# Two layers of attention and a routed feed-forward network: six additions of softmax tiles moved from GpSimd to VectorE, with four edits at the kernel's end

## The chip, the cores and the metric

The kernel runs on one core of one Trainium2 chip. The core has a matrix engine (TensorE, in the profile PE, with its weight loads shown as PEld), an elementwise engine (VectorE, DVE), an engine for activations (ScalarE, ACT), a general engine (GpSimd, POOL) and one that mostly issues transfers (SyncE, SP). Each works through its own list of instructions in order and waits on semaphores for the others. Sixteen DMA engines move data; SP, ACT and POOL issue transfers to them.

The metric is the device time of one execution in microseconds (us), lower is better. Three runs of the kernel before took 4557.66 to 4558.62 us, with a median of 4558.31.

## The reference

The input x has 2048 tokens of 1024 numbers. Two layers follow each other, with the same weights:

```python
    def _A_ref(x, wqkv, wo):
        ...                       # H = 32 heads of 32
        scores = jnp.einsum("bhqd,bhkd->bhqk", q, k) * scale
        p = _softmax(scores, axis=-1)
        o = jnp.einsum("bhqk,bhkd->bhqd", p, v)
        return (lambda x, *d: x.transpose(*d))(o, 0, 2, 1, 3).reshape(B, S, D) @ wo

    def _B_ref(x, w_r, w_gate, w_up, w_down):
        r = x @ w_r
        idx = jnp.argsort(-r, axis=-1)[:, :C]          # the 8 tokens with the largest r
        ...
        g = _silu(x_sel @ w_gate)
        u = x_sel @ w_up
        y = (g * u) @ w_down                           # 1024 -> 3584 -> 1024, 8 tokens only
        r_sel = _sigmoid(jnp.take_along_axis(r, idx, axis=1))
        y = y * r_sel.reshape(B, C, 1)
        ...                                            # y is added to those 8 rows
    x = x + _A_ref(_layernorm(x, axis=-1), A_wqkv, A_wo)
    x = x + _B_ref(_layernorm(x, axis=-1), B_w_r, B_w_gate, B_w_up, B_w_down)
    x = x + _A_ref(_layernorm(x, axis=-1), A_wqkv, A_wo)
    x = x + _B_ref(_layernorm(x, axis=-1), B_w_r, B_w_gate, B_w_up, B_w_down)
```

So each layer is full attention over 2048 tokens, then a router that picks 8 tokens for a gated feed-forward network.

## The kernel before, in words

**Attention.** After a normalisation and the projections, attention is cut into 32 units (8 groups of four heads, by 4 chunks of 512 queries). A unit has 16 steps, one for each tile of 128 keys, so there are 512 steps in a layer. A step computes scores (PE, L703), takes their exponential (ACT, L1099) into a tile P of 128 by 2048, and one or two steps later multiplies P with the values (PE, L1025). A separate product and reduction find each row's maximum ahead of time (PE L688, DVE L696); it runs 25 steps ahead of the exponentials, and so VectorE's large reductions end 25 steps before the last step.

**The softmax's sums.** The 16 P tiles of a unit must be summed. Five times a tile is added onto another by a transfer that accumulates, issued by GpSimd (`merge`, L1038). Eight tiles are added into a buffer `acc` by GpSimd (`acc_add`, L1035). At step 22 counted from the unit's start (in the next unit, `SUM_AT`) PE multiplies two P tiles and `acc` by ones (`sum_mm`, L1045), and ACT copies the result (L1055). When each of these happens is written in tables:

```python
MERGED = ((2, 0), (8, 6), (11, 8), (13, 10), (15, 12))
ADDED = ((5, 3), (6, 0), (9, 5), (12, 4), (14, 6), (15, 8), (16, 10), (20, 12))
```

The first number is the step from the unit's start, the second the tile; a merge adds the next tile onto it. Thus tiles 6, 8, 10 and 12 are added after their merges. P tiles live in nine buffers, and an exponential waits until its buffer's last reader is done. In the last unit of a layer there are no merges: VectorE makes 12 adds and three tiles go directly to the sum.

**Output projection.** It works in 16 row tiles of 128 tokens (PE L1238). Each tile t has a scaling of the attention output by the sums' reciprocals (`scale_o`, L1161 on VectorE, L1170 and L1173 for the split into two parts), the products, a sum with x (L1243), a normalisation (L1271) and the router's logits (L1273, which writes its product into the accumulator that the products came from). In layer 1 the last two row tiles, 14 and 15, are computed apart from the others (L1303) with parts of the router's work called in between; `row_sums` (L1312, L1315) and `logits` (L1320, L1321) finish them. The row tile 15 is scaled in row tile 12's turn.

**The routed network in layer 1.** `finish` runs 49 steps: eight gate steps and eight up steps for the first half of the network's width, a transposition (L548), the same for the second half, fourteen down steps (L563), and the output y (L578), which GpSimd scatters to the tokens' rows (L579). Gate and up products are L531. After each gate, up and down step SP issues the next weights' load (L204, L207). Gate results go through ACT (L538, L539), VectorE (L540, L541) and GpSimd (L542) before VectorE multiplies them with the up results (L544).

**The moving-back.** Some rows had been exchanged with others so that the router could work on a part of the tokens early. `back(i)` gathers eight rows (GpSimd, L216), loads eight others (ACT's queue) and scatters both groups (GpSimd, L220) to where they belong. In `choose`, `back(1)` is called at the end, which is after step 2; `back(0)` follows after step 9. GpSimd's queue takes these in program order.

Of the kernel before, what the change touches and what calls it, by code (L numbers as in the profile page):

```python
# [19 lines left out]
NT = S // 128  # L20
# [3 lines left out]
NU = NG * QC  # L24
# [13 lines left out]
ADDED = ((5, 3), (6, 0), (9, 5), (12, 4), (14, 6), (15, 8), (16, 10), (20, 12))  # L38
FIRST = 2
# [8 lines left out]
KEYS_AT[3, 3] = slice(3 * 512, S)  # L48


def unit_events(last):
    if last:
        return [(k + 1, "mid", 1, "add", (k, 0 if k == 1 else None, True)) for k in range(1, NT) if k not in LAST_DIRECT]
    ev = [(at, "end", 0, "merge", (k, k + 1)) for at, k in MERGED]
    ev += [(at, "end", 1, "add", (k, FIRST if at == ADDED[0][0] else None, False)) for at, k in ADDED]
    return ev + [(SUM_AT, "mid", 5, "sum", ())]


EVENTS = {False: unit_events(False), True: unit_events(True)}


@with_exitstack
def tile_kernel(ctx, tc, x, wqkv, wo, w_r, w_gate, w_up, w_down, out):
    nc = tc.nc
    sync, dve, act, pool, pe = nc.sync, nc.vector, nc.scalar, nc.gpsimd, nc.tensor
# [15 lines left out]
    def ps_st():  # L81
        return psum.tile([128, 512], F32, name="st", bufs=3)
# [4 lines left out]
    def ps_pv():  # L87
        return psum.tile([128, 512], F32, name="pv")
# [23 lines left out]
    pos = cons.tile([128, NT], F32, name="pos")  # L112
# [30 lines left out]
    def ln_stats(xt, st=None):  # L143
        if st is None:
            st = small.tile([128, 2, 6], F32, name="bst", bufs=3)
            for i in range(2):
                dve.bn_stats(st[:, i, :], xt[:, i * 512:(i + 1) * 512])
        mv = small.tile([128, 2], F32, name="mv", bufs=3)
        dve.bn_aggr(mv, st)  # L149
        rs = small.tile([128, 1], F32, name="rs", bufs=3)  # L150
        pool.tensor_tensor(rs, mv[:, 1:2], eps_c, op=OP.add)  # L151
        pool.tensor_tensor(rs, rs, mhalf, op=OP.pow)
        return mv, rs

    class FeedForward:
# [67 lines left out]
        def tiny(self, shape, name, dtype=F32):  # L223
            return small.tile(shape, dtype, name=name, bufs=1)
# [152 lines left out]
        def back(self, i):  # L377

            end, perm = (CUT + 8, S)[i], PERM[i]
            rows, last = (self.tmp.tile([128, D], F32, name=k, bufs=b)[0:8] for k, b in (("x", 3), ("wrb", 1)))  # L380
            self.gather(rows, perm["ab"][:, 1:2], self.dst)
            act.dma_start(last, self.dst[end - 8:end, :])
            self.scatter(perm["ab"][:, 0:1], rows, self.dst)
            self.scatter(perm["routed"], last, self.dst)

        def token(self, s):

            j = small.tile([64, 8], F32, name="tj")
            for i in (1, 0):
                a, b, t, bc = self.tiny([64, 1], "ta"), self.tiny([64, 1], "tb"), self.tiny([64, 1], f"tt{i}"), PERM[i]["bc"]  # L390
                dve.scalar_tensor_tensor(j, bc[:, 0:8], s, bc[:, 8:16], op0=OP.is_equal, op1=OP.mult, accum_out=a)
                dve.scalar_tensor_tensor(j, tails[i], s, bc[:, 16:24], op0=OP.is_equal, op1=OP.mult, accum_out=b)
                dve.tensor_tensor(a, a, b, op=OP.add)
                dve.tensor_tensor(t, a, s, op=OP.add)
                s = t
            return s
# [83 lines left out]
        def choose(self):  # L480

            tiny, f = self.tiny, self.final
            mx, mi, mif = tiny([1, 8], "mx1"), tiny([1, 8], "mi", U32), tiny([1, 8], "mif")
            dve.max(mx, f)
            dve.max_index(mi, mx, f)
            dve.tensor_copy(mif, mi)
            yield
            p = ps_st()
            pe.matmul(p[0:64, 0:8], ones_c[0:1, 0:64], mif, start=True, stop=True)
            tables = (self.cand, last_c[0], last_c[1])  # L490
            for j, t in enumerate(tables):
                pe.matmul(p[0:64, 16:25], self.pk[0:t.shape[0], j, :], t, start=(j == 0), stop=(j == 2))
            eq, away, tab = tiny([64, 8], "eq64"), tiny([64, 1], "away"), tiny([64, 9], "tab")
            dve.tensor_scalar(eq, p[0:64, 0:8], col_c, None, op0=OP.is_equal)
            dve.tensor_copy(tab, p[0:64, 16:25])
            dve.tensor_reduce(away, eq, axis=AX.X, op=OP.max)
            dve.tensor_scalar(away, away, -4.0 * S, 4.0 * S, op0=OP.mult, op1=OP.add)
            place, idx, tok = tiny([64, 1], "place64"), tiny([64, 1], "idx64", I32), tiny([64, 1], "tok64", I32)
            dve.scalar_tensor_tensor(place, tab[:, 0:1], 2.0, half_c, op0=OP.mult, op1=OP.add)
            dve.tensor_copy(idx, place)  # L500
            halves = self.halves = self.dst.rearrange("s (b c) -> (s b) c", b=2)
            self.gather(self.bg, idx, halves)

            t = self.token(tab[:, 0:1])
            dve.scalar_tensor_tensor(place, t, 2.0, half_c, op0=OP.mult, op1=OP.add)
            dve.tensor_tensor(place, place, away, op=OP.add)
            dve.tensor_copy(tok, place)
            self.tok = tok
            sg = self.sg = tiny([64, 1], "sg64")
            act.activation(sg, tab[:, 8:9], AF.Exp, scale=-1.0)  # L510
            dve.tensor_scalar(sg, sg, 1.0, None, op0=OP.add)
            dve.reciprocal(sg, sg)
            self.back(1)
            yield

        def row_tile(self):
# [2 lines left out]
        def step(self):  # L519
# [3 lines left out]
            k, h, a = u = self.steps.pop(0)  # L523
            nj = 4 - h
            m = 32 * nj
            if k in "gu":
                if a == 0:
                    self.acc = ps_pv()
                w = self.W.pop(u)
                for j in range(nj):  # L530
                    pe.matmul(self.acc[32 * j:32 * j + 32, :], self.xs[:, a, :], w[:, j * 512:(j + 1) * 512],  # L531
# [65 lines left out]
            self.lag = 0  # L597

        def finish(self):
            choice = self.choose()  # L600
            for i in range(len(self.steps)):
                if self.step():
                    if self.free:
                        self.pools.append(self.free.pop(0))
                    self.load()
                if i in (0, 2):
                    next(choice)
                if i == 9:
                    self.back(0)
            self.close()  # L610

        def close(self):
# [19 lines left out]
    def layer(n, src, dst, prev=None, following=None):  # L632
# [93 lines left out]
        with ExitStack() as pst:  # L726
# [209 lines left out]
            for k, (c, wb, i) in enumerate(steps):  # L936
# [26 lines left out]
                at = b - (1, 8)[c == 0]  # L963
                t = 4 * (c + 1) + at // 4
# [30 lines left out]
        with sbuf(f"at{n}", bufs=2) as aw:  # L995
# [79 lines left out]
            def emit(s, where):  # L1075
                u, kt = divmod(s, NT)
                todo = []
                for back in (1, 0):
                    v = u - back
                    if 0 <= v < NU:  # L1080
                        todo += [(kt + NT * back, pri, fn, args, v) for (k, pos, pri, fn, args) in EVENTS[v == NU - 1]
                                 if k == kt + NT * back and pos == where]
                for k, _, fn, args, v in sorted(todo, key=lambda e: (-e[0], e[1])):
                    fns[fn](v, *args)
# [5 lines left out]
            for s in range(NS + 14):  # L1090
                u, kt = divmod(s, NT)
# [10 lines left out]
                t = s - 1 if s < NS - LEAD else s - 2  # L1102
# [39 lines left out]
        if True:  # L1142
# [17 lines left out]
            def scale_o(t):  # L1160
                dve.tensor_tensor(OR[t], OR[t], RD.pop(t), op=OP.mult)  # L1161
# [61 lines left out]
            for t in range(NT - 2 if n else NT):  # L1223
# [27 lines left out]
                mv, rs = ln_stats(x2)  # L1251
                if low:
                    low()
                if n and t == NT - 4:
                    scale_o(NT - 1)
                if first_stage and t == CT + 3:
                    list(first_stage)
                    next(nxt)
# [12 lines left out]
                dve.tensor_scalar(xn, x2, mv[:, 0:1], rs, op0=OP.subtract, op1=OP.mult)  # L1271
                waste = wp.tile([128, D], F32, name="x", bufs=3) if nxt and t == NT - 1 else p
                dve.scalar_tensor_tensor(waste, xn, 1.0, wrb, op0=OP.mult, op1=OP.mult, accum_out=rcols[:, t:t + 1])  # L1273
                if nxt and NT - 3 <= t < NT - 1:
                    next(nxt)
                pool.tensor_tensor(x2, x2, xn, op=OP.add)
# [9 lines left out]
        if n:  # L1286

            parts = ffn.first_rows(rcols)
# [4 lines left out]
            todo = [(i, x, wol, a, both) for i, x in ((0, ah), (1, bh)) for a in range(KD)]  # L1293
# [14 lines left out]
            def row_sums(i, between=None):  # L1308
                st = small.tile([128, 2, 6], F32, name="bst", bufs=3)
                for h in both:  # L1310
                    o = x2s[i][:, halves[h]]
                    dve.tensor_tensor(o, p[i][h], o, op=OP.add)  # L1312
                    if between and h == 0:
                        next(between)
                    dve.bn_stats(st[:, h, :], o)  # L1315
                mvs[i], rss[i] = ln_stats(None, st)

            def logits(i):
# [12 lines left out]
            xns = [wp.tile([128, D], F32, name="xn", bufs=1), more[:, 0:D]]  # L1331
            last = [ffn.last_rows(1 + i, rcols[:, NT - 2 + i:NT - 1 + i], xns[i]) for i in both]
            row_sums(0)
            next(parts)
            pool.memset(ffn.pk, 0.0)
# [15 lines left out]
            for i in range(2):  # L1351
                t = NT - 2 + i
# [40 lines left out]
```

## Time and profile before

| | us |
|---|---|
| three runs, median (lowest to highest) | 4558.31 (4557.66 to 4558.62) |
| the profiled execution, its time | 4557.8 |
| its span, first to last instruction | 4556.0 |
| PE busy | 4506.4 |
| GpSimd busy | 3231.7 |
| VectorE busy | 3150.2 |
| ScalarE busy | 2428.5 |

A row of a timeline reads: start in the span, busy time, engine, line of the kernel, operation, what it writes and reads, how many instructions the row stands for, and in brackets how long the engine was idle before and what ended that. L numbers are lines of the kernel before. Names such as `ohl`, `wol`, `fw` or `xn` are buffers that serve several uses one after another; in the routed network they hold weights or intermediate results. Layer 1's attention ends near 4284 us and its routed network starts near 4478 us.

### The profile page before, as it was taken

To read this page: it belongs to the slowest core of one execution; us is meant where nothing else is said; L and a number is where in the kernel's file an instruction comes from. 1 tells how busy PE (TensorE), PEld (TensorE's weight loads), DVE (VectorE), ACT (ScalarE), POOL (GpSimd) and SP (SyncE) were. 2 spreads that over 40 slices of the span, in tenths; PEclk is the share of its full clock that TensorE was granted. 3 is DMA by queue.
4 is the path that set the end of the run, shared out by engine and by line. 5 is a ranking of instruction groups with operands and counts; after the bars stand their busy time and mean duration, and the time that the engine had idled before them with its cause. 6 is when DMAs were issued, how large, how long until landed. Compare 5 with 4: busy or idle time off the path is not lost.

```text
span 4556.0 us, 73559 instructions
## 1 busy us (share of the span) xinstructions
PE 4506.4 (99%) x29241; PEld 2686.4 (59%) x29241; DVE 3150.2 (69%) x4963; ACT 2428.5 (53%) x2574; POOL 3231.7 (71%) x1251
## 2 busy tenths in 40 slices
PE   9999999999999999999999999999999999999997
PEld 7888745555555555548877786555555555555583
DVE  2211588888888888876522225888888888888663
ACT  3322267767676767670222222767777676767510
POOL 4444378989898889855633343888989898989452
PEclk9999999999999999999999999999999999999998
DMA  6757477777777768758698774877777777777598
GB/s 206 210 171 207 130 170 154 171 156 160 167 163 158 172 145 180 168 122 242 183 318 279 252 207 122 175 153 166 164 152 174 157 160 167 164 158 175 140 277 322
DMA packets 329719, 833.62 MB, mean 183 GB/s; under 512 B 43996, under 2 KB 160732, under 8 KB 280206
## 3 DMA queue, kind: packets, MB, share of 16 engines
q1 hardware_dynamic: 275454, 476.43, 35.4%
q0 software_dynamic: 45248, 325.67, 35.3%
q10 hardware_dynamic: 8672, 26.81, 2.2%
q8 instruction: 230, 3.77, 0.3%
q14 instruction: 115, 0.94, 0.1%
HBM read 384.34 MB, written 119.47 MB: 111 GB/s over the span
## 4 chain that ended last, share of the span: by engine, by line
PE 94%; DMA 2%; POOL 1%; issue 1%; DVE 1%; ACT 0%; ACTq 0%; POOLq 0%; SPq 0%; DVEq 0%
PE pv L1025 22%; PE pre L703 21%; PE st L821 17%; PE st L688 16%; PE pre L821 6%; PE pre L1238 5%; PE st L1045 4%; POOL acc L1035 1%; PE pv L531 1%; PE pre L688 1%; PE pv L821 0%; PE pre L790 0%; DMA ord<-rd 0%; PE st L571 0%; PE pre L1303 0%
## 5 line engine op out<-in xcount | busy, mean ns | idle before, releaser
L696 DVE TENSOR_REDUCE nm<-st 128x1 f32<-128x512 f32 x3916 | 2434.0, 684 | 376.1 <-PE st L688 370.1
L1099 ACT ACTIVATE P<-pre 128x1024 f32<-128x1024 f32 x2048 | 1985.9, 1022 | 723.3 <-PE pre L703 521.4
L1035 POOL TENSOR_TENSOR acc<-acc,P 128x2048 f32<-128x2048 f32 x434 | 2103.9, 4848 | 86.2 <-DMA P<-P 75.4
L703 PE MATMUL pre<-q,ks 64*128 64x512 f32 (+1 forms) x8192 | 1142.4, 396 | 4.3 <-ACT P L1099 4.3
L1025 PE MATMUL pv<-P,v 128*32 128x512 f32 x8192 | 1092.8, 606 | 4.8 <-DMA v<-vd 4.8
L688 PEld LDWEIGHTS st<-ks,q 64*128 64x128 f32 x3916 | 547.0, 184 | 907.4 <-DVE nm L696 764.9
L688 PE MATMUL st<-ks,q 64*128 64x512 f32 x3916 | 985.9, 471 | 0.5
L703 PEld LDWEIGHTS pre<-q,ks 64*128 64x128 f32 (+1 forms) x8192 | 776.1, 187 | 186.0 <-ACT P L1099 57.4
L1038 POOL DMA_DIRECT2D P<-P x310 | 296.8, 957 | 260.0 <-PE st L688 189.3
L836 DVE TENSOR_TENSOR lo<-st,hi 128x512 fp32r<-128x512 f32 x128 | 88.4, 692 | 528.4 <-ACT hi L835 505.2
L756 POOL TENSOR_TENSOR ohl<-wraw,ord 128x2048 fp32r<-128x2048 f32 (+1 forms) x54 | 222.5, 4124 | 308.1 <-ACT ord L751 299.5
L756 POOL TENSOR_TENSOR wl<-wraw,wh 128x2048 fp32r<-128x2048 f32 (+1 forms) x54 | 222.4, 4122 | 303.7 <-ACT wh L755 284.9
L835 ACT CAST hi<-st 128x512 fp32r<-128x512 f32 x128 | 75.2, 587 | 496.5 <-PE st L821 493.3
L1025 PEld LDWEIGHTS pv<-P,v 128*32 128x32 f32 x8192 | 162.5, 108 | 261.3 <-issue 253.6
L1035 POOL TENSOR_TENSOR acc<-P 128x2048 f32<-128x2048 f32 x62 | 294.0, 4742 | 11.0 <-ACT P L1099 11.0
L1238 PE MATMUL pre<-woh,ohl 128*128 128x512 f32 x960 | 223.2, 390 | 0.0
L1238 PEld LDWEIGHTS pre<-woh,ohl 128*128 128x128 f32 x960 | 180.0, 188 | 39.6 <-ACT ohl L1170 1.7
L821 PE MATMUL st<-xh,wh 128*128 128x512 f32 x512 | 201.4, 393 | 0.0
L821 PE MATMUL st<-xh,wl 128*128 128x512 f32 x512 | 199.6, 390 | 0.0
L821 PE MATMUL st<-xl,wh 128*128 128x512 f32 x512 | 199.5, 390 | 0.0
L151 POOL TENSOR_TENSOR rs<-mv,eps_c 128x1 f32<-128x1 f32 x64 | 29.3, 457 | 232.2 <-DVE mv L149 232.2
L1170 ACT CAST ohl<-ord 128x1024 fp32r<-128x1024 f32 x32 | 33.6, 1052 | 269.9 <-DVE ord L1161 115.7
(384 smaller groups left out, 3995.7 us busy)
## 6 DMA issues: line engine op xcount, KB each, us to landing
P<-P POOLq DMA_DIRECT2D x310, 1024.0 KB, 8.8
wraw<-in_A_wqkv_dram SPq DMA_DIRECT2D x96, 1024.0 KB
q<-qh SPq DMA_DIRECT2D x256, 128.0 KB
ks<-kh SPq DMA_DIRECT2D x112, 256.0 KB
fw<-in_B_w_down_dram SPq DMA_DIRECT2D x17, 1024.0 KB
vd<-vn SPq DMA_DIRECT2D x32, 512.0 KB
qh<-hi SPq DMA_DIRECT2D x64, 256.0 KB
ql<-lo SPq DMA_DIRECT2D x64, 256.0 KB
```

Of the source, the lines that this page charges most:

```text
L688: pe.matmul(ps[b], Q[u][rows, i, 0, qt * 128:(qt + 1) * 128], KS[(u // QC) % 2][rows, i, 0, j * 512:(j + 1) * 512], start=True, stop=True, ...
L696: dve.tensor_reduce(NM[u][:, j, 2 * i + b:2 * i + b + 1, qt], ps[b], axis=AX.X, op=OP.max, negate=True)
L703: pe.matmul(p[:, b * 512:(b + 1) * 512], KS[(u // QC) % 2][rows, i, slot, kt * 128:(kt + 1) * 128], Q[u][rows, i, slot, :], start=(slot == ...
L756: pool.tensor_tensor(wl[:, sl], raw[:, sl], wh[:, sl].bitcast(F32), op=OP.subtract)
L821: pe.matmul(p, *pair(a, l, r), start=(a == 0 and k == 0), stop=(a == KD - 1 and k == 2))
L836: dve.tensor_tensor(lo, p, hi.bitcast(F32), op=OP.subtract)
L1025: pe.matmul(PV[u][32 * h:32 * h + 32, :], V[g][:, kt, 32 * h:32 * h + 32], P[s][:, h, :], start=(kt == 0), stop=(kt == NT - 1), tile_posit ...
L1035: (dve if on_dve else pool).tensor_tensor(o, a, P[u * NT + k].rearrange("p h c -> p (h c)"), op=OP.add)
L1038: pool.dma_start(P[u * NT + a], P[u * NT + b], accum_op=OP.add)
L1045: pe.matmul(p[32 * h:32 * h + 32, :], ones32, a[:, h, :], start=(i == 0), stop=(i == len(parts) - 1), tile_position=(0, 32 * h))
L1099: act.activation(P[s][:, 2 * i:2 * i + 2, :].rearrange("p h c -> p (h c)"), p, AF.Exp, scale=SCALE)
L1238: pe.matmul(p[:, bl], l[:, a, :], r[a][:, bl], start=(k == 0 and a == 0), stop=(k == 2 and a == KD - 1))
```

## The change

1. `unit_events` takes the number of units that are left. For the last unit but one (`left == 1`), the adds at steps 9 and later, six of eight, are made by VectorE instead of GpSimd. This holds in both layers.
2. `back` becomes a generator with two parts (gather and load; scatters). `choose` no longer calls it. `finish` runs `back(1)`'s parts after steps 3 and 8, and `back(0)`'s after steps 17 and 25.
3. In layer 1, the up steps accumulate in the pool `ps_st` instead of `ps_pv`, which the gate steps use.
4. In layer 1, `scale_o` of row tile 15 moves behind row tile 12's normalisation and logits.
5. In `row_sums`, each half's statistics are taken directly after its sum, ahead of the router's part that is called in between.

```diff
+ON_DVE = 9
...
-def unit_events(last):
-    if last:
+def unit_events(left):
+
+    if left == 0:
         return [(k + 1, "mid", 1, "add", (k, 0 if k == 1 else None, True)) for k in range(1, NT) if k not in LAST_DIRECT]
     ev = [(at, "end", 0, "merge", (k, k + 1)) for at, k in MERGED]
-    ev += [(at, "end", 1, "add", (k, FIRST if at == ADDED[0][0] else None, False)) for at, k in ADDED]
+    ev += [(at, "end", 1, "add", (k, FIRST if at == ADDED[0][0] else None, left == 1 and at >= ON_DVE)) for at, k in ADDED]
     return ev + [(SUM_AT, "mid", 5, "sum", ())]
...
-EVENTS = {False: unit_events(False), True: unit_events(True)}
+EVENTS = [unit_events(i) for i in range(3)]
...
             act.dma_start(last, self.dst[end - 8:end, :])
+            yield
             self.scatter(perm["ab"][:, 0:1], rows, self.dst)
             self.scatter(perm["routed"], last, self.dst)
+            yield
...
             dve.reciprocal(sg, sg)
-            self.back(1)
             yield
...
                 if a == 0:
-                    self.acc = ps_pv()
+                    self.acc = ps_st() if self.n and k == "u" else ps_pv()
...
         def finish(self):
-            choice = self.choose()
+            choice, backs = self.choose(), [self.back(i) for i in range(2)]
+
+            parts = {0: choice, 2: choice, 3: backs[1], 8: backs[1], 17: backs[0], 25: backs[0]}
             for i in range(len(self.steps)):
...
-                if i in (0, 2):
-                    next(choice)
-                if i == 9:
-                    self.back(0)
+                if i in parts:
+                    next(parts[i])
...
-                        todo += [(kt + NT * back, pri, fn, args, v) for (k, pos, pri, fn, args) in EVENTS[v == NU - 1]
+                        todo += [(kt + NT * back, pri, fn, args, v) for (k, pos, pri, fn, args) in EVENTS[min(NU - 1 - v, 2)]
...
-                if n and t == NT - 4:
-                    scale_o(NT - 1)
...
                 dve.scalar_tensor_tensor(waste, xn, 1.0, wrb, op0=OP.mult, op1=OP.mult, accum_out=rcols[:, t:t + 1])
+                if n and t == NT - 4:
+                    scale_o(NT - 1)
...
                     dve.tensor_tensor(o, p[i][h], o, op=OP.add)
+                    dve.bn_stats(st[:, h, :], o)
                     if between and h == 0:
                         next(between)
-                    dve.bn_stats(st[:, h, :], o)
```

## The prediction

> **What bounds the kernel now.** I read the page first, then a table of the engines' work by stretches of the span, then the instruction rows of each engine around the places that the diff touches. The page gives the span and says which engine carries the end.
>
> ```profile
> span 4556.0 us, 73559 instructions
> PE 4506.4 (99%) x29241; PEld 2686.4 (59%) x29241; DVE 3150.2 (69%) x4963; ACT 2428.5 (53%) x2574; POOL 3231.7 (71%) x1251
> PE 94%; DMA 2%; POOL 1%; issue 1%; DVE 1%; ACT 0%; ACTq 0%; POOLq 0%; SPq 0%; DVEq 0%
> ```
>
> TensorE is busy 4506.4 of 4556.0 us, so only some 50 us can be won by removing waits, and a removed wait pays only if TensorE has no other wait behind it. The table by stretches shows where that holds (stretch, length, busy time of PE, PEld, DVE, ACT and POOL, granted clock, DMA share, GB/s).
>
> ```profile
> 4288.00:4440.00 152.00, 152.00 (x670) 125.36 (x668) 104.56 (x128) 20.15 (x20) 73.59 (x91) 1.00 0.94 261
> 4475.00:4500.00 25.00, 20.06 (x149) 7.30 (x148) 7.45 (x30) 1.28 (x3) 6.29 (x7) 0.84 0.86 309
> 4500.00:4530.00 30.00, 24.95 (x142) 7.27 (x144) 6.40 (x6) 1.06 (x2) 6.05 (x6) 0.89 1.03 400
> ```
>
> Layer 1's output projection (4288 to 4440) has no gap in PE: what attention gains ahead of it arrives behind it. In the routed network at the end (from 4475) PE has gaps, and from 4500 the DMA engines have none: there the weights' transfers bound the work, not PE.
>
> **Attention, layer 0.** The rows of PE, then of ScalarE, then of GpSimd in time order around the last unit but one's sum, then one unit's sum without a wait from the chain of work, and layer 1's two rows that frame the same place:
>
> ```profile
> 1998.77 1.38 PE L703 MATMUL pre<-q,ks 64*128 64x512 f32 x8
> ...
> 2002.03 0.74 PE L703 MATMUL pre<-q,ks 64*128 64x512 f32 x4 [0.88 <-ACT P L1099]
> ...
> 2004.50 1.90 PE L1045 MATMUL st<-P,ones 128*32 128x512 f32 x16
> 2007.53 1.07 PE L1045 MATMUL st<-acc,ones 128*32 128x512 f32 x8 [1.13 <-POOL acc L1035]
> ...
> 2011.17 1.38 PE L703 MATMUL pre<-q,ks 64*128 64x512 f32 x8
> ...
> 2026.80 1.24 PE L703 MATMUL pre<-q,ks 64*128 64x512 f32 x8
> ...
> 2000.96 1.94 ACT L1099 ACTIVATE P<-pre 128x1024 f32<-128x1024 f32 x2 [1.59 <-POOL acc L1035]
> 2007.51 1.94 ACT L1099 ACTIVATE P<-pre 128x1024 f32<-128x1024 f32 x2 [4.61 <-POOL acc L1035]
> ...
> 1988.96 18.52 POOL L1035 TENSOR_TENSOR acc<-acc,P 128x2048 f32<-128x2048 f32 x3
> ...
> 2889.30 2.58 PE st L1045 x24
> ...
> 4251.61 1.40 PE L703 MATMUL pre<-q,ks 64*128 64x512 f32 x8
> ...
> 4264.04 1.40 PE L703 MATMUL pre<-q,ks 64*128 64x512 f32 x8
> ```
>
> GpSimd's last three adds end at 1988.96 + 18.52 = 2007.48. The sum's last eight matmuls start at 2007.53 and an exp that needs the last added tile's buffer at 2007.51. So GpSimd is the engine that holds both. The seven steps from 2011.17 to 2026.80 take 15.63/7 = 2.233 us each. From 1998.77 to 2011.17 lie three steps and one sum, 12.40 us; undisturbed these are 3 × 2.233 + 2.58 = 9.28. The loss is 3.12 us, and in layer 1 (4264.04 − 4251.61 = 12.43) 3.15.
>
> **What the move to VectorE does.** Six adds per layer (P5, 4, 6, 8, 10, 12) leave GpSimd for VectorE. The rows of VectorE's and GpSimd's adds and of the four merges that GpSimd issues here:
>
> ```profile
> 1992.67 3.81 DVE L1035 TENSOR_TENSOR acc<-P 128x2048 f32<-128x2048 f32 x1 [10.30 <-ACT P L1099]
> ...
> L1035 DVE TENSOR_TENSOR acc<-acc,P x11: 2291/2293/6497, 1996.6 to 2028.9; 128x2048 f32<-128x2048 f32 x11
> ...
> L1035 POOL TENSOR_TENSOR acc<-acc,P x6: 4869/5358/6532, 1973.1 to 2001.0; 128x2048 f32<-128x2048 f32 x6
> L1038 POOL DMA_DIRECT2D P<-P x4: 874/1320/1677, 1972.5 to 1988.0; - x4
> ...
> DMA to landing us min/median/max: 7.4/8.4/8.6
> ```
>
> An add costs VectorE 2.29 us alone (the median) against GpSimd's 4.87 to 6.53. The slow ones on both engines are those that ran at the same time; afterwards GpSimd has no adds there, so I price all of VectorE's at 2.29. VectorE was idle for the 10.30 us before 1992.67, so it has the room. The order on its queue becomes P5, 4, 6, 8, a reciprocal, 10, then the last unit's adds 1, 2, 3, then 12, then 4 to 12. Adds 6, 8, 10 and 12 each wait for a merge's landing, and whatever is queued behind a waiting add waits with it: that is the added risk. The last merge was issued at 1988.0 and landed at most 8.6 later, 1996.6. On GpSimd the merges no longer stand behind adds, so I take them as issued, and landing, no later than now. The third then landed around 1991.3 (spacing (1988.0 − 1972.5)/3 = 5.2 before the last). Add 10 runs 1991.3 to 1993.6, add 1 to 1995.9. Adds 2 and 3 wait for exps of two more steps (1992.67 + 2 × 2.233 = 1997.1 for the third), so 3 ends at 1999.4 to 2000.5; add 12 follows, its merge already landed, and ends by 2002.8. PE, without the wait ahead of the sum, starts the sum 0.88 earlier and wants this add after 16 of its 24 matmuls, at 2004.50 − 0.88 + 2.58 × 16/24 = 2005.3: 2.5 us to spare. The buffers that the two exps wait for come free earlier too. So the whole stall goes: **3.1 per layer, 6.2 in all**; bounds 0 (a late merge eats it) and 6.4. The last unit's remaining adds also end earlier (nine at 2.29 from 2002.8 give 2023.4, where now 34.6 us of adds end at 2031).
>
> **Row 12's scaling, layer 1.** PE, then VectorE:
>
> ```profile
> 4436.28 3.79 PE L1238 MATMUL pre<-wol,ohl 128*128 128x512 f32 x16
> 4441.16 3.88 PE L1303 MATMUL pre<-wol,ohl 128*128 128x512 f32 x16 [1.09 <-ACT ohl L1170]
> ...
> 4437.74 1.23 DVE L1161 TENSOR_TENSOR ord<-ord 128x1024 f32<-128x1024 f32 x1 [3.46 <-DMA ord<-rd]
> ...
> 4439.72 1.23 DVE L1273 SCALAR_TENSOR_TENSOR pre<-xn,wrb 128x1024 f32<-128x1024 f32 x1
> ```
>
> The profile names a ScalarE cast as what ended PE's 1.09 us. But the first product writes the accumulator that row 12's logit operation (L1273) reads, and that ends at 4439.72 + 1.23 = 4440.95, just ahead of 4441.16. It stood behind the scaling of row 15, which waited 3.46 us for its load. Moved behind it, the scaling holds nothing that PE needs soon, and L1273 fits into those 3.46 us. **Gain 1.09**; bounds 0 (the cast after all) and 1.09.
>
> **Statistics before the pick.** VectorE, then PE, in the last rows' sums:
>
> ```profile
> 4466.00 0.23 DVE L470 TENSOR_SCALAR ohl<-st,pos 128x8 f32<-128x8 f32 x1 [0.70 <-PE st L468]
> 4466.15 0.68 DVE L1315 BATCH_NORM_STATS2 bst<-x 128x6 f32<-128x512 f32 x1
> ...
> 4470.43 0.37 PE L459 MATMUL st<-ident,rcols 128*1 128x128 f32 x1 [2.19 <-DVE rcols L1321]
> ```
>
> The statistics (0.68) fit into the 0.70 in which VectorE waited for the pick's matmul; the pick is then some 0.1 late, which PE does not feel in its 2.19 of waiting. The second half's add then starts behind the pick, at 4466.00 + 0.23, instead of behind the statistics, at 4466.15 + 0.68: 0.6 earlier, of which I take **0.55**; bounds 0 and 0.7.
>
> **The routed network.** PE, VectorE and GpSimd rows, then the DMA rates of 4475 to 4556 in 40 slices of 2.03 us with the weight queue's bytes:
>
> ```profile
> 4489.49 1.93 PE L531 MATMUL pv<-fw,xs 128*32 128x512 f32 x16 [1.19 <-ACT xn L539]
> ...
> 4503.00 1.11 PE L548 MATMUL st<-ident,xn 128*128 128x128 f32 x4 [6.43 <-DVE xn L544]
> ...
> 4513.70 6.21 PE L531 MATMUL pv<-fw,xs 128*32 128x512 f32 x42 [1.18 <-ACT xn L539]
> ...
> 4539.31 7.04 PE L563 MATMUL st<-fw,ht 128*32 128x512 f32 x32
> ...
> 4502.25 0.69 DVE L544 TENSOR_TENSOR xn<-pv,xn 128x512 f32<-128x512 f32 x1 [9.37 <-POOL xn L542]
> ...
> 4500.06 0.86 POOL L220 DMA_INDIRECT out_dram<-wrb,routed  x1 [4.70 <-DMA out_dram<-x,ab]
> ...
> GB/s 115 216 286 270 288 243 360 332 309 422 413 414 414 422 404 414 386 279 409 411 405 407 409 417 405 407 419 403 409 419 403 398 417 218 2 0 16 0 0 0
> ...
> q1 hardware_dynamic: 5445, 23.48, 75.6%
> ```
>
> The split of the moving-back lets GpSimd multiply the first gate half (L542) before the scatters, where it now runs behind the one at 4500.06; that ends VectorE's 9.37 and PE's 6.43. The accumulators in the other pool end the 1.19 and the 1.18. Together 8.80 us of PE's waiting go. But the rates stand at about 410 GB/s from the tenth slice (4493) to the 33rd (4541.8), and the weights' bytes do not shrink. The last of them move in the 34th slice, 218/410 of it, so until 4542.9; the last step of the down projection starts at 4539.31 + 7.04 × 3/4 = 4544.6 and its second half 0.9 later. PE can come forward only by the distance from landing to use, between 0 and 2.6 us. I take **0.8** of 8.80, as a landing comes some time after the bytes move. To this belongs that the stream starts with the gate steps, which come 1.09 + 0.55 earlier; that shift is already in the sum.
>
> Sum: 6.2 + 1.09 + 0.55 + 0.8 = 8.64 us. The profiled execution took 4557.8 (1.8 around its span), which gives 4549.2; it lies 0.5 under the median of 4558.31, from which the same sum gives 4549.7. I work from the middle of both, 4558.05, here and for the rivals: **4549.4**, its own range 4547.5 to 4551.
>
> **Rivals.**
> (a) *The stream does not hold PE.* If the loads also start earlier when the up steps lose their 1.19, and the low slice at 4509.4 (279 for 410, 0.65 us) fills up, the tail gains 1.8 more: 4547.6. If PE's waits were the bound outright, 8.0 more: 4541.4. For it: the slices ahead of 4493 run at 243 to 360 GB/s. Against it: the 24 slices of full rate. Chance 0.2, nearly all for the smaller.
> (b) *The clock falls in the down projection.* A step there takes 7.04/4 = 1.76 us of PE, and a megabyte at 410 GB/s 2.56 us; with its reserve gone PE would be busy 69%. In 4475 to 4500, with PE busy 20.06 of 25.00, the granted clock was 0.84. If the clock halves, a step takes 3.5 us, and the last one or two steps end 1.8 to 3.5 later: 4551.2 to 4552.9. Chance 0.2. The Trainium skill ("TensorE: Matmul & The Clock Gate", HAM oscillation) describes just this: compute shorter than the wait for the next slice of weights, and a clock that drops at each; by its window of about 3.4 us a wait of 0.8 alone would not suffice, and no run here shows yet such a sequence.
> (c) *Attention's stall only moves.* If merges, no longer spaced by adds, compete and land 2.5 + 3.1 us later than I take, the sum waits as long as now: only 2.44 stays, 4555.6. For it: four issues of which each needs 5 us or more of transfer. Against it: earlier issue. Chance 0.13.
> (d) *VectorE becomes the slower adder*, which ends on the other side. Between the third merge and the sum it has five adds in line (10, 1, 2, 3, 12). At 2.29 they leave 2.5 us; at the 3.81 of the row at 1992.67 they end 5 × 1.52 = 7.6 later, and the stall is 5.1 instead of 3.1, +4.0 in two layers, less 2.44: 4559.6. At 6.5, the slowest row, they end 21.1 later, a stall of 18.6 and so 4586.6. Slower than before from (2.5 + 3.1 + 1.2)/5 = 1.36 above 2.29, 3.65 us an add. Against it: those rows are of adds beside GpSimd's, which are gone. Chance 0.07.
>
> **How the numbers follow.** The forecast has 0.40. Below 4546 I leave little but the large form of (a), above 4554.5 (c)'s full form and (d): the range is 4546 to 4554.5. What a measurement can tell from no change is 0.2%, 9.1 us, so the border is 4549.2, within the forecast's own range. Faster by more: nearly half of the forecast (0.18), all of (a) (0.2) and 0.06 for a shift of the stretches in which the clock is below 1.00 (0.84 and 0.89 above), which can fall either way: 0.44. Slower by over 0.2%: (d) from about 4.6 us an add, where it passes 4567, and what lies beside these cases, 0.06. Within: 0.50.
>
> **What would show it.** In the changed profile: no GpSimd add in the waits of ScalarE and PE at the last unit but one, and 9.3 us for the three steps with the sum; VectorE's adds at 2.29; PE's 1.09 before L1303 gone; PE's waits of 6.43, 1.19 and 1.18 gone, but new waits on weights of about 0.8 us a step in the down projection, at a full clock. Wrong would be: an add on VectorE waiting for a merge while the sum waits for it, a clock below 1.00 in the down projection, or an end that follows PE's 8.80.

## The result, and the profile after

| | before | after |
|---|---|---|
| median of 22 runs each, us | 4559.39 | 4552.27 |
| lowest to highest, us | 4553.04 to 4564.80 | 4548.57 to 4557.77 |
| profiled execution: time, span, us | 4557.8, 4556.0 | 4548.81, 4547.0 |

The ratio is 0.9985, with a 95% interval of 0.9979 to 0.9991: faster by 4 to 10 us. The gain is 7.1 us where 8.64 were forecast. The median lies inside the prediction's range of 4546 to 4554.5, but 2.9 us above the forecast of 4549.4 and 1.3 above what the prediction called its own range. The profiled execution of after lies 3.5 us under its own median, so each term is read from rows, and from more than one profile where it matters.

The page of the kernel after, its span, busy times and chain of work:

```profile
span 4547.0 us, 73545 instructions
PE 4503.8 (99%) x29241; PEld 2681.0 (59%) x29241; DVE 3159.2 (69%) x4975; ACT 2429.3 (53%) x2574; POOL 3168.8 (70%) x1239
PE 96%; DMA 1%; DVE 1%; issue 1%; POOL 0%; ACT 0%; SPq 0%; POOLq 0%; ACTq 0%; DVEq 0%
```

Twelve adds went from POOL (1251 to 1239 instructions) to DVE (4963 to 4975), six in each layer. (Line numbers after are 4 to 7 higher: L703 is L709, L1035 is L1041, L1045 is L1051, L1273 is L1277, L1303 is L1309.)

Attention after, rows of PE for layer 0's three steps with the sum, layer 1's first and fourth step, and the start of layer 1's projection:

```profile
1997.52 1.34 PE L709 MATMUL pre<-q,ks 64*128 64x512 f32 x8
...
2001.89 1.90 PE L1051 MATMUL st<-P,ones 128*32 128x512 f32 x16
2003.60 1.04 PE L1051 MATMUL st<-acc,ones 128*32 128x512 f32 x8
...
2006.71 1.43 PE L709 MATMUL pre<-q,ks 64*128 64x512 f32 x8
...
4247.38 1.35 PE L709 MATMUL pre<-q,ks 64*128 64x512 f32 x8
...
4256.58 1.43 PE L709 MATMUL pre<-q,ks 64*128 64x512 f32 x8
...
4279.97 0.73 PE L1244 MATMUL pre<-woh,ohl 128*128 128x512 f32 x2 [0.35 <-ACT ohl L1176]
4281.23 7.12 PE L1244 MATMUL pre<-woh,ohl 128*128 128x512 f32 x30 [0.53 <-DVE ohl L1179]
...
4433.76 3.79 PE L1309 MATMUL pre<-wol,ohl 128*128 128x512 f32 x16
```

The three steps take 9.19 and 9.20 us instead of 12.40 and 12.43, and the sum's matmuls run without a wait. The last rows' products (4433.76) wait for nothing: the 1.09 is gone. But there are two waits that the kernel before didn't have, 0.35 and 0.53 us at the start of layer 1's projection. From the fourth step to the last rows' products it took 4441.16 − 4264.04 = 177.12 us before and takes 4433.76 − 4256.58 = 177.18 now. So over this stretch nothing was won: what the last rows gained, the start lost.

VectorE's adds of tiles 6, 8 and 10 after, then the row that holds the last unit's, with tile 12's as the third in it:

```profile
1978.99 2.29 DVE L1041 TENSOR_TENSOR acc<-acc,P 128x2048 f32<-128x2048 f32 x1 [8.86 <-DMA P<-P]
1985.39 2.29 DVE L1041 TENSOR_TENSOR acc<-acc,P 128x2048 f32<-128x2048 f32 x1 [4.11 <-DMA P<-P]
...
1990.30 2.29 DVE L1041 TENSOR_TENSOR acc<-acc,P 128x2048 f32<-128x2048 f32 x1 [0.95 <-DMA P<-P]
...
1994.89 28.26 DVE L1041 TENSOR_TENSOR acc<-acc,P 128x2048 f32<-128x2048 f32 x12
```

Each add takes 2.29 us; three wait for a merge's landing, and all end in time for the sum. So rival (d) did not occur. Of rival (c) a part did: the merges are issued up to 2.1 us earlier against the steps than before, but take longer to land. The view of GpSimd's transfers there, after (the prediction has that of before, 7.4/8.4/8.6):

```profile
DMA to landing us min/median/max: 7.5/9.7/10.5
```

So they land where they did, between 0.6 us later and 0.2 earlier, and the sum does not wait.

The routed network after, PE's rows, then two stretches of the down projection (columns as in the prediction):

```profile
4470.02 5.07 PE L537 MATMUL pv<-fw,xs 128*32 128x512 f32 x24 [0.32 <-DVE xs L483]
...
4487.91 0.66 PE L554 MATMUL st<-ident,xn 128*128 128x128 f32 x4 [0.88 <-DVE xn L550]
...
4505.14 0.71 PE L554 MATMUL st<-ident,xn 96*128 96x96 f32 x4 [2.70 <-DVE xn L550]
4505.78 3.39 PE L569 MATMUL st<-ord,ht 128*32 128x512 f32 x8
...
4518.41 1.91 PE L569 MATMUL st<-woh,ht 128*32 128x512 f32 x8 [0.66 <-DMA woh<-in_B_w_down_dram]
...
4533.74 3.63 PE L569 MATMUL st<-fw,ht 128*32 128x512 f32 x16 [0.64 <-DMA fw<-in_B_w_down_dram]
```

```profile
4509.00:4521.00 12.00, 10.70 (x52) 2.48 (x49) 0.00 (x0) 0.00 (x0) 0.87 (x1) 1.00 1.03 410
4521.00:4537.00 16.00, 12.78 (x56) 2.73 (x56) 0.00 (x0) 0.00 (x0) 0.00 (x0) 1.00 0.87 347
```

The waits of 6.43, 1.19 and 1.18 are gone, and the down steps begin 35.8 us after the gate steps instead of 44.2. The first six find their weights there; then come seven waits for weights, of 0.56 to 0.74 us. From the first gate step to the last down step it is 67.35 us (4470.02 to 4533.74 + 3.63) against 68.42 before.

### The profile page after: what moved, and what is told of

The parts are those of the page before. It is cut to its first block, busy times and chain, and to the rows that moved or that the text cites. A ratio compares the mean times of both kernels' runs of the same rounds, so it can differ in the third digit from the quotient of the medians.

```text
span 4547.0 us, 73545 instructions
## 1 busy us (share of the span) xinstructions
PE 4503.8 (99%) x29241; PEld 2681.0 (59%) x29241; DVE 3159.2 (69%) x4975; ACT 2429.3 (53%) x2574; POOL 3168.8 (70%) x1239
## 4 chain that ended last, share of the span: by engine, by line
PE 96%; DMA 1%; DVE 1%; issue 1%; POOL 0%; ACT 0%; SPq 0%; POOLq 0%; ACTq 0%; DVEq 0%
PE pv L1031 23%; PE pre L709 21%; PE st L827 17%; PE st L694 16%; PE pre L1244 6%; PE pre L827 5%; PE st L1051 4%; PE pv L537 1%; PE pre L694 1%; PE pv L827 0%; PE pre L796 0%; DMA wraw<-in_A_wqkv_dram 0%; PE st L577 0%; PE pre L1309 0%; DMA v<-vd 0%
## 5 line engine op out<-in xcount | busy, mean ns | idle before, releaser
L1041 POOL TENSOR_TENSOR acc<-acc,P 128x2048 f32<-128x2048 f32 x422 | 2038.0, 4829 | 87.3 <-DMA P<-P 80.5
L709 PE MATMUL pre<-q,ks 64*128 64x512 f32 (+1 forms) x8192 | 1141.4, 396 | 1.7 <-ACT P L1105 1.7
L709 PEld LDWEIGHTS pre<-q,ks 64*128 64x128 f32 (+1 forms) x8192 | 773.2, 186 | 184.1 <-ACT P L1105 51.4
L1041 POOL TENSOR_TENSOR acc<-P 128x2048 f32<-128x2048 f32 x62 | 294.6, 4752 | 9.6 <-ACT P L1105 9.6
L1176 ACT CAST ohl<-ord 128x1024 fp32r<-128x1024 f32 x32 | 33.6, 1051 | 271.8 <-DVE ord L1167 87.8
```

Of the source, the lines that this page charges most:

```text
L709: pe.matmul(p[:, b * 512:(b + 1) * 512], KS[(u // QC) % 2][rows, i, slot, kt * 128:(kt + 1) * 128], Q[u][rows, i, slot, :], start=(slot == ...
L1041: (dve if on_dve else pool).tensor_tensor(o, a, P[u * NT + k].rearrange("p h c -> p (h c)"), op=OP.add)
```

## The experiments

**The first edit alone, and the other four alone.** On the kernel before, and on the changed one:

```diff
 # the first edit alone: before, with
-    ev += [... (k, FIRST if at == ADDED[0][0] else None, False) ...]
+    ev += [... (k, FIRST if at == ADDED[0][0] else None, left == 1 and at >= ON_DVE) ...]
 # the other four alone: after, with
-    ev += [... left == 1 and at >= ON_DVE ...]
+    ev += [... False ...]
```

> The kernel before with the first edit alone (six adds of the last unit but one made by VectorE, both layers). If GpSimd's late adds were the stall, the three steps with the sum take 9.3 us in each layer instead of 12.4, and the time falls by about 6.2 us (ratio 0.9986). If the stall only moves to a merge or to VectorE's queue, the three steps stay near 12.4 and the time stays within 1 us.

> The changed kernel without the first edit (the adds on GpSimd again, the four edits at the end kept). If the parts add up, the three steps take 12.4 us again and the time is about 2.4 us under that of before (ratio 0.9995). If the end's edits were the larger part, it is 4 us or more under it.

The first edit alone: median 4553.96 of 11 runs against 4558.49 of 27, ratio 0.9989 (0.9980 to 0.9998); the three steps take 9.19 and 9.20 us. The other four alone: 4557.46, ratio 0.9998 (0.9989 to 1.0007); the three steps take 12.34 and 12.47. With the changed kernel's 0.9986 on the same chip (below), 4.5 and 1.0 us against 6.6 for all, so the parts add up within their intervals. Each is smaller than its terms in the sum (6.2 and 2.44), and the second can't be told from no change by its times. The rows of the second show where a part of the first was lost:

```profile
4262.96 1.40 PE L709 MATMUL pre<-q,ks 64*128 64x512 f32 x8
...
4438.82 3.56 PE L1309 MATMUL pre<-wol,ohl 128*128 128x512 f32 x15
```

From attention's step 504 (the fourth step above) to the last rows' products, the four kernels take, in us:

| | adds on GpSimd | adds on VectorE |
|---|---|---|
| scaling of row 15 as before | 177.12 (before) | 177.43 (first edit alone) |
| scaling of row 15 moved | 175.86 (the other four) | 177.18 (after) |

With the adds on GpSimd, the moved scaling gives its 1.09 and a little more: 1.26. With them on VectorE the projection starts late, and PE reaches the last rows no earlier than the unmoved scaling lets it: the moved scaling then gives only 0.25, and in the first edit alone the wait ahead of the last rows is gone too. So the first edit gives 1.3 us back in layer 1's projection where the scaling is moved, and only 0.3 where it is not. These are two delays on parallel paths, and taking away one of them is worth little while the other stays. The table has one profile of each kernel; a second of after gives 177.26, and a second of before 179.24, with a wait of 1.27 in the projection that the first does not have.

**Both kernels once more.** Nothing is changed in either.

> The changed kernel unchanged, for a second profile. The first profiled execution lies 3.5 us under the median of its 22 runs. If that is chance in places that the change does not touch (where the clock falls, a gap in an engine's own issue), the differences of the two profiles lie there, and the three steps with the sum again take 9.3 us and the tail after the gate steps' start 67.4 us. If the tail itself varies, the two profiles differ behind the gate steps' start.

> The kernel before, unchanged, for a second profile. The three steps with the sum take 12.4 us in both layers, PE waits 1.09 us ahead of the last rows' products, and 6.4, 1.2 and 1.2 us in the routed network, if these waits belong to the program; what differs between the two profiles of before is the size of what a single profile cannot tell.

After: 4551.88 of 11 runs, ratio 0.9986 (0.9977 to 0.9995). Before: one run, 4560.15. The stall and the waits at the projection's start came out the same in each pair, and those in the routed network and ahead of the last rows within 0.5 us (before: 5.93 for 6.43, 1.43 for 1.09). What differs lies elsewhere: from the gate steps' start to the end of the down steps 67.35 and 68.53 after, 68.42 and 67.34 before; and from the first to the last product of layer 1's projection, before, 152.7 and 154.5. The first expected value, 67.4 for the tail, was missed by 1.1: the tail varies too, by more than the 0.8 that was to be found there. The second profile of before names the wait ahead of the last rows as the prediction read it:

```profile
4444.54 1.62 PE L1303 MATMUL pre<-wol,ohl 128*128 128x512 f32 x6 [1.43 <-DVE pre L1273]
```

**The two waits at the projection's start.** ScalarE's rows there, after:

```profile
4276.74 1.05 ACT L1205 CAST woh<-wor 128x1024 fp32r<-128x1024 f32 x1
4278.87 1.04 ACT L1176 CAST ohl<-ord 128x1024 fp32r<-128x1024 f32 x1 [1.09 <-issue]
```

Before, the cast of the first split tile followed the one ahead of it without a gap, 0.96 us before the sum's 24th matmul ended:

```profile
4285.24 1.04 ACT L1170 CAST ohl<-ord 128x1024 fp32r<-128x1024 f32 x1
```

Now the cast that PE waits for starts 1.09 us late, and the profile names no releaser. The view of the line L1176 after shows a wait of the engine's queue ahead of it, of 2.57 us:

```profile
L1176 ACTq EVENT_SEMAPHORE  x1: 2572/2572/2572, 4276.3 to 4276.3; - x1
```

It ends at 4278.83, and the last of the sum's 24 matmuls that read P tiles ends at 4278.76. All eight profiles of kernels with the moved adds and without the exchange below have this queue wait and the gap, and the cast starts 0.11 us behind the 24th matmul in each (from attention's step 504 to the projection's first product they take 23.4 us); none of the four without the moved adds has either (22.95). The theory is that it comes from where the tiles lie: P tiles take whichever buffer came free, and with the adds on VectorE that order changed. By the built program, the last P tile of layer 1 now lies at the address at which the first split tile `ohl` is put, so the cast must wait until the sum has read P. The traces hold no addresses, so an experiment has to bear this out; it exchanges the first two split tiles:

```diff
             load_o(0, sync)
+            if n:
+                OT[1] = halves_o()
+                pool.memset(OT[1][0][:, 0, 0:1].bitcast(F32), 0.0)
             OT[0] = halves_o()
...
-                    OT[1] = halves_o()
+                    if not n:
+                        OT[1] = halves_o()
```

> The changed kernel with the first two split tiles of the output projection in layer 1 exchanged in memory (a one-column memset claims the other place first). Theory: in layer 1 the last P tile of attention now lies where the first split tile is written, so ScalarE's cast of it waits 1.09 us for the sum's matmuls that read that P tile, and PE waits 0.35 + 0.53 us at the projection's start. Then the gap of 1.09 us on ScalarE is gone, PE has no wait there, and from attention's step 504 to the last rows' products it takes 1.0 to 1.3 us less (176.0 instead of 177.2); the time falls by about 1.2 us against the changed kernel. Rival: the gap is a delay of the engine's own issue; then it stays, and the 177.2 with it.

ScalarE's and PE's rows with the exchange:

```profile
4278.04 1.05 ACT L1208 CAST woh<-wor 128x1024 fp32r<-128x1024 f32 x1
4278.98 1.05 ACT L1176 CAST ohl<-ord 128x1024 fp32r<-128x1024 f32 x1
```

```profile
4279.88 1.04 PE L1051 MATMUL st<-acc,ones 128*32 128x512 f32 x8
4280.85 7.67 PE L1248 MATMUL pre<-woh,ohl 128*128 128x512 f32 x32
...
4303.99 6.37 PE L1248 MATMUL pre<-woh,ohl 128*128 128x512 f32 x27 [0.80 <-DVE pre L1281]
```

The gap, the queue's wait and both of PE's waits are gone. From attention's step 504 to the start of PE's 32nd product it takes 30.3 us, as before, instead of the changed kernel's 31.4. So it was no delay of the engine's own issue, and the start's loss of 1.1 us is recovered. It does not stay: a wait of 0.80 us later on, which the changed kernel's first profile doesn't have, takes part of it (to the last rows' products 176.79, not 176.0), and the last rows then take 2.0 us longer (see the next experiment). In this profile the gate steps start 215.2 us after step 504, in the changed kernel's three between 213.4 and 213.9. Time: 4550.74 of 11 runs, ratio 0.9982 (0.9973 to 0.9991), 1.1 and 1.5 us under the changed kernel's medians so far; the intervals overlap, so the rows show the cause, but no gain of the whole kernel is shown.

**Scaling beside GpSimd.** Where row 15's scaling now stands, the profiles show something else. VectorE, then GpSimd, after:

```profile
4431.14 2.88 DVE L1167 TENSOR_TENSOR ord<-ord 128x1024 f32<-128x1024 f32 x1 [0.54 <-DMA ord<-rd]
```

```profile
4430.53 2.39 POOL L1282 TENSOR_TENSOR x<-x,xn 128x1024 f32<-128x1024 f32 x1
```

The scaling took 1.23 us where it stood before; here it ends 1.10 us after GpSimd's addition (4430.53 + 2.39 = 4432.92, 4431.14 + 2.88 = 4434.02), as if it had begun almost only then. The next version leaves the explicit scaling out, so that the splitting does it one row later:

```diff
 # besides the exchange
-                if n and t == NT - 4:
-                    scale_o(NT - 1)
```

> The changed kernel with the exchanged split tiles and without the explicit scaling of row tile 15 (it is then scaled when it is split, in row tile 13's turn, behind the next sum and so clear of GpSimd's addition). If VectorE's 2.9 to 3.4 us for that scaling in four of seven profiles are a wait for GpSimd's addition that began first, it takes 1.2 us here, PE's wait ahead of the last rows' products stays at 0.2, and the last rows take 24.1 us; the time is 1 to 1.5 us under the changed kernel's beside it. If the scaling's length has another cause, it is over 2 us again.

> The changed kernel once more, on the same chip as the version before it, so that the two can be compared. About 1 to 1.5 us slower than that one if its two edits are worth what the profiles say, and 6 to 7.5 us faster than before.

The scaling took 1.22 us, as expected, and 3.27 in the changed kernel beside it, again with GpSimd's addition under way. But the last rows, to the start of their last product, took 25.1 us, not 24.1 (24.0 before): it now stands ahead of row 13's statistics, and PE waits 0.78 us for the logits behind them. Time: 4551.16 against 4553.89, 11 runs each on the same chip, ratios 0.9985 (0.9976 to 0.9994) and 0.9988 (0.9979 to 0.9997). The medians lie 2.7 us apart, more than the 1 to 1.5 expected, but the two intervals overlap, and the rows of the two profiles show no gain: from attention's step 504 to the gate steps they take 213.9 us in both. So the two edits of this version are not shown to be worth anything together; what the exchange won, the scaling's new place lost.

**What bounds the tail.** Half of each down step's weights are not loaded in these two; its first 128 rows are used twice:

```diff
-                for i in [slice(0, 1), slice(1, 2)] if self.n and a == 13 else [slice(0, 2)]:
+                for i in [slice(0, 1)] if self.n else [slice(0, 2)]:
...
-                                      w[:, i * D + b * 512:i * D + (b + 1) * 512],
+                                      w[:, b * 512:(b + 1) * 512],
```

> The changed kernel with half of the down projection's weights not loaded (each down step uses the first 128 of its 256 rows twice), so 7.3 MB less in the stream with the same matmuls. If the stream bounds the end, PE's waits of 0.65 us a down step go and the end comes some 5 us earlier, then bound by PE. If PE or the clock bounds it, less than 1 us changes.

> The kernel before with half of the down projection's weights not loaded (each down step uses the first 128 of its 256 rows twice). The changed kernel took 58.6 us so from the gate steps' start to the end of the down steps. If the stream is what kept the four edits' gain in the tail near nothing, the kernel before takes 7 us or more longer than that here, about 66 to 67.5 us, with its waits of 6.4, 1.2 and 1.2 us in place. If the edits save no time on PE's own path, it takes 60 us or less.

PE's rows, changed kernel with half the weights:

```profile
4472.58 3.65 PE L537 MATMUL pv<-fw,xs 128*32 128x512 f32 x20 [0.32 <-DVE xs L483]
...
4524.18 7.04 PE L569 MATMUL st<-fw,ht 128*32 128x512 f32 x32
```

and kernel before with half the weights:

```profile
4478.98 5.08 PE L531 MATMUL pv<-fw,xs 128*32 128x512 f32 x24 [0.32 <-DVE xs L476]
...
4503.94 1.11 PE L548 MATMUL st<-ident,xn 128*128 128x128 f32 x4 [6.54 <-DVE xn L544]
...
4540.20 7.04 PE L563 MATMUL st<-fw,ht 128*32 128x512 f32 x32
```

With half the weights the changed kernel's tail takes 58.6 us and that of before 68.3, as with all of them. The four edits save 9.6 us on PE's path; with all the weights the stream gives back all but some tenths. The gain from halving the bytes was 9 us in the changed kernel, not the 5 expected. Against its first profile, 5.8 came from the seven waits (a step with one took 2.55 us, a step without 1.72), 1.5 from the first down step, which ran at half clock there and at full clock here, and 1.4 from an earlier start of the down steps.

**The second moving-back later.**

```diff
-            parts = {... 17: backs[0], 25: backs[0]}
+            parts = {... 33: backs[0], 37: backs[0]}
```

> The changed kernel with the second moving-back after steps 33 and 37 instead of 17 and 25. If SP's wait of 8.8 us for its load's landing thins out the weights' stream, that wait and the low slices (370 and 301 GB/s) go, ScalarE's gate exponential of the second half is no longer 2.8 us late behind that load, and from the gate steps' start to the end of the down steps it takes about 0.7 us less than the 67.4 to 68.5 of two profiles of the changed kernel. If the queue of loads covers SP's wait, it stays within them.

```profile
4507.71 0.55 PE L554 MATMUL st<-ident,xn 96*128 96x96 f32 x4 [0.87 <-DVE xn L550]
4508.21 1.91 PE L569 MATMUL st<-ord,ht 128*32 128x512 f32 x8
4510.68 1.91 PE L569 MATMUL st<-wol,ht 128*32 128x512 f32 x8 [0.56 <-DMA wol<-in_B_w_down_dram]
```

The wait of 2.70 in the changed kernel was ScalarE's queue: the split-off load at step 17 waits for a scatter, and the second gate half's exponential stands behind it. The exponential after:

```profile
4498.50 0.59 ACT L544 ACTIVATE xn<-pv 96x512 f32<-96x512 f32 x1 [17.20 <-DMA out_dram<-wrb,routed]
```

Moved, the wait is 0.87 and the first down step runs at full clock. The down steps then wait for weights from the second step on, and the tail takes 67.8 us (gate steps from 4475.38 on), within the changed kernel's two values. SP still waited 4.3 us for the split-off load to land, where it had waited 8.8. So the stream covers these waits, as the second half of the expectation had it; the 0.7 did not come.

**VectorE's margin.** An operation of an add's size is put in once, then twice, ahead of the add of tile 10:

```diff
+                for _ in range(1 if u == NU - 2 and k == 10 else 0):     # then 2
+                    dve.tensor_tensor(o, o, o, op=OP.max)
```

> The changed kernel with one more operation of an add's size on VectorE ahead of the add of tile 10, in both layers (the larger of the accumulator and itself, which changes nothing). By the prediction's margin of 2.5 us it costs nothing; by the changed kernel's profile, where the add of tile 12 ends about 2001.9 and the sum uses it at 2003.6, the margin is 1.7 us and the three steps with the sum take 9.2 + 0.6 us in each layer. If VectorE has no margin, they take 2.3 us more.

> The changed kernel with two more operations of an add's size ahead of the add of tile 10, in both layers. One of them cost nothing. If the margin is the prediction's 2.5 us, two cost 4.5 - 2.5 = 2.0 us in each layer (the three steps take 11.2 us) and the sum waits for VectorE. If the margin is over 4.5 us, they take 9.2 us again.

```profile
2006.59 1.07 PE L1053 MATMUL st<-acc,ones 128*32 128x512 f32 x8 [1.61 <-DVE acc L1043]
```

One costs nothing: the three steps take 9.20 and 9.21 us. With two they take 11.13 and 11.14, and the sum waits for VectorE. Two operations of 2.2 to 2.3 us and a loss of 1.93 leave a margin of 2.5 to 2.7 us. It has two parts: the add of tile 12 ends 1.8 us before the sum uses it (2001.78 and 2003.60), and VectorE waits 0.95 for the third merge, which the added operations fill. The expectation of 1.7 left out the second part.

## Why the prediction was right, and where it was off

- *Attention's stall.* 3.1 per layer forecast, 3.21 and 3.23 measured: the mechanism and the size were right. The margin that kept rival (d) away was 2.5 us from the end of tile 12's add to its use in the prediction. In these terms it is 1.8; that the experiment's 2.5 to 2.7 agrees is partly luck, as it includes the wait for a merge. The merges landed as the prediction took them to, within 0.6 us, but only because an earlier issue made up for a longer way to landing.
- *"What attention gains ahead of it arrives behind it."* This step failed in layer 1. That the projection showed no gap said nothing of how much room ScalarE's cast ahead of it had: the change moved a P tile under the cast's output, the cast came 1.1 us later against the sum, and PE started late. The trace of before cannot show that; it hangs on which buffer the last P tile gets. Of layer 1's 3.2 us, 1.1 are lost by PE's 32nd product and 1.3 by the last rows, where the scaling is moved. In layer 0 PE starts its projection without a wait.
- *Row 12.* 1.09 forecast, 1.26 measured with the adds on GpSimd, but 0.25 with them on VectorE. DVE, not the cast that the profile named, is the releaser, as the prediction read it. What it did not price is that the moved scaling meets GpSimd's addition, in all nine profiles that have it there. In six the scaling is held up (2.9 to 3.4 us), in three the addition; in four of the six the last rows took 0.1 to 0.5 us longer than before, in the other two (the exchange, and two added operations) 1.9 to 2.0.
- *Statistics before the pick.* 0.55 forecast. From the start of the last product of the last rows to the gate steps it took 12.74 in all four profiles with the old order, and 12.14 to 12.53 in the ten with the new one, 12.28 in the mean: 0.46 less.
- *The tail.* 0.8 forecast out of 8.80. The mechanism was right and shown with half the weights, so rival (a), that the stream does not hold PE, is out. The size can't be told from scatter: in eight profiles with the four edits and all the weights the tail takes 67.19 to 68.53 us, 67.87 in the mean; in three without, 67.34 to 68.64, 68.13 in the mean. That is 0.26.
- *The clock, rival (b).* In the prediction's terms a clock below 1.00 in the down projection would have been a sign of its being wrong. It fell, in the first profile of after, for the first step (3.39 us for eight matmuls, 1.91 at full clock; granted clock 0.79 from 4501 to 4509), behind a wait of 2.70, and this the stream covered: with the moving-back later the first step ran at full clock and the tail took 67.83. From 4509 to 4537 the clock stayed at 1.00, though PE was busy only 80 to 89%. All eight profiles of the tail named above have a slow first step, behind waits of 2.54 to 3.53; with half the weights a wait of 2.50 left it at full clock. The Trainium skill ("TensorE: Matmul & The Clock Gate", HAM oscillation) has the clock fall for waits that cross its window; the trace agrees in that waits of 0.65 did not do it. It differs in that waits of 2.54 to 3.00, shorter than that window of about 3.4, did. The prediction took the page's case for just this one, which it was not: there the compute is shorter than the wait, here a step of 1.72 us stands beside a wait of 0.65, and in the prediction one of 1.76 beside 0.8.

Summed: 3.21 + 3.23 in attention, 1.26 − 1.32 in the projection, 0.46 for the statistics and 0.26 in the tail make 7.1 us, as much as the medians of the 22 runs differ by. That it fits to a tenth is luck, as the runs' interval is 4 to 10 us and the last term lies within its scatter. Against the 8.64 forecast, 1.5 us are missing: 1.15 in layer 1's projection, 0.5 in the tail and 0.1 in the statistics, less 0.24 that attention gave in addition.

## What to carry to other kernels

Before a stall's gain is carried through a stage that shows no gap, look for what in that stage has little time to spare, and for which memory the next stage's first tiles take over. A move between engines can change the order in which buffers come free, and with it which tile lies under which; a gap that the profile puts down to "issue" may be such a wait. Where a transfer stream is at its full rate, as from 4493 to 4542 in the kernel before, price removed waits by the distance from landing to use, and halve the bytes in an experiment to see what they were worth.

## What was not expected of the hardware

VectorE and GpSimd held each other up almost completely, in the order in which they began. With two operands in SBUF, the scaling (1.22 alone) took 2.88, 3.27 and 3.41 us when GpSimd's addition had begun first, and ended 1.1 us after it. In the profile with the exchange:

```profile
4432.37 3.43 POOL L1286 TENSOR_TENSOR x<-x,xn 128x1024 f32<-128x1024 f32 x1 [1.91 <-DVE xn L1279]
```

```profile
4433.48 3.41 DVE L1167 TENSOR_TENSOR ord<-ord 128x1024 f32<-128x1024 f32 x1
```

GpSimd's addition takes 2.39 alone and 3.43 here, where VectorE was at work on another operation when it began; VectorE's scaling, which came later, ends 1.09 us after it (4435.80, 4436.89). In the three profiles in which the scaling began first, by 0.1 us, it took its 1.22 and the addition 3.39 to 3.41. So the later of the two loses all but 0.13 us of the time for which they overlap. The Trainium skill ("SBUF — State Buffer", SBUF: two separate sides) says that of a GpSimd operation that reads SBUF and a VectorE operation with two SBUF inputs the one that starts first holds a shared pair of ports for the whole instruction and the other is blocked; the trace agrees, and adds the price. The 3.81 and 6.5 us adds of before fit it: the first began at 1992.67, beside an addition of GpSimd's that ended at 1994.31, and ended 2.16 us after that, where an add alone takes 2.29.
